# Moving the tiles that TensorE streams to one address residue in an attention and two-layer MoE kernel

## The chip, the cores and the metric

The kernel runs on one core of a Trainium2 chip. The time is the device time of one execution in microseconds (us). TensorE (PE) does the matrix multiplications; each is a weight load (LDWEIGHTS, engine row PEld) of the stationary operand and a MATMUL that streams the moving operand through it into PSUM. VectorE (DVE), ScalarE (ACT) and GpSimd (POOL) do the rest, SyncE (SP) issues the DMAs. SBUF, the working memory, has 128 partitions; an address below is a byte within a partition.

## The reference

All is computed in float32 (the weights are drawn as float64 and come in as pairs of 32-bit words).

```
attention: batch 2, 8 heads, 768 positions, head size 64
  scores = q k^T / 8 within |i-j| < 16, beside q kmax^T / 8 + log 32 for the 24 blocks of 32 keys
  a = softmax over both;  x = a [v, mean of v by block]          -> 1536 tokens x 512
moe:   h = relu(x @ w_in);  y = (h * h) @ w_out                  w_in 512 x 2048, w_out 2048 x 512
moe2:  h = y @ w_in2;  e = exp(h - max);  s = h * e / (sum e + 1e-9)
       ln = (s - mean) / sqrt(var + 1e-6) * g;  out = ln @ w_out2   w_in2 512 x 1024, w_out2 1024 x 512
```

## The kernel before, in words

To keep float32 precision, each operand of a large product is split in two parts of type float32r, a high part (`xh`, `gh`, `yh`, `lh`, and half 0 of a weight tile) and what is left (`xl`, `gl`, `yl`, `ll`, half 1). A product is then three matmuls: high by high, high by low, low by high.

The 1536 tokens are three tiles of 512. A string, `ORDER`, sets by hand in which order every engine gets its work; the letters M, U, G, D, O name the five stages of one step of the first MoE layer. There are 48 steps: 3 token tiles by 16 chunks of 128 hidden columns.

- M, `mm1` (line 466): 12 matmuls into one PSUM bank `h`. Stationary are slices of `wi`, 128 columns each; moving are `xh`, `xl`, 512 columns each, in the order xh, xl, xh for each quarter of the 512 inputs.
- U, G, D: the ReLU into `r`, the squares `gh` (line 481) and `r` (line 482) on ACT, and `gl` = r - gh on DVE or POOL (line 89).
- O, `mm2` (line 495): 12 matmuls into four PSUM banks `acc`, three in each. Stationary are slices of `wo`; moving are gh, gl, gh.

The attention of tokens tiles still to come (lines 181 to 360) lies between the first steps, until about 162 us. The weights come by DMA as 64-bit words into `st`, are put together as float32 in `wf` by ACT and DVE (letters a to e), and split into the ring `wp` (`wi`, `wo`; letters F, f). The weights of the second MoE layer go through the same path: ten 128 x 2 x 512 tiles into `w2` of a pool `rp` that is opened once the attention's tiles are given back, the next two into a `wi` slot of the ring, the last six into `wo` slots.

The second layer works on 12 blocks of 128 tokens, in the function `moe2`:

- `ysplit` (ACT, POOL) makes `yh`, `yl` in slots of `wf`;
- `mm3` (line 541): 2 x 12 matmuls into two banks; stationary are slices of yh, yl, moving are eight `w2` tiles (named `w` in the profile);
- `solu` (lines 548 to 566): a chain over DVE, ACT and POOL;
- `ln_tr` (line 578): 8 transposes, and the split into `lh`, `ll`;
- `mm4` (line 601): 24 matmuls into one bank `po`. Stationary are lh, ll; moving are the weights: 6 matmuls with `w2` (`w` in the profile), 6 with the ring slot `wi`, 12 with `wo`. The last block does it in two halves of 256 columns.

Tiles come from pools. A pool of the left side is put behind the one opened before it; pools of the right side are put down from the end of the memory. `gp` holds r, gh, gl (two slots each) and the small tiles of `solu` (three slots each). Tiles start on multiples of 32 bytes.

Of the kernel before, what the change touches and what calls it, by code (L numbers as in the profile page):

```python
# [12 lines left out]
F32 = mybir.dt.float32  # L13
# [46 lines left out]
def attn_moe_kernel(ctx, tc, q, k, v, w_in, w_out, w2_in, w2_out, g_ln, out):  # L60
# [5 lines left out]
    P = 128  # L66
# [28 lines left out]
    one = cp.tile([P, 1], F32, name="one")  # L95
    g_sb = cp.tile([P, NF2], F32, name="g_sb")

    gp = ctx.enter_context(tc.tile_pool(name="gp", bufs=3))
    yp = ctx.enter_context(tc.tile_pool(name="yp", bufs=1))
    wp = ctx.enter_context(tc.tile_pool(name="wp", bufs=RING))  # L100
    stp = ctx.enter_context(tc.tile_pool(name="stp", bufs=3))
# [15 lines left out]
    rctx = ExitStack()  # L117
    ctx2 = ExitStack()
    rp = {}
# [424 lines left out]
    def solu(i):  # L544
        h2 = h2_t.pop(i)
        yhl.pop(i)
        nm = gp.tile([P, 1], F32, name="nm")
        nc.vector.reduce_max(out=nm, in_=h2, axis=AX.X, negate=True)  # L548
        e = stp.tile([P, DF2], F32, name="st")
        s = gp.tile([P, 1], F32, name="s2")  # L550
        nc.scalar.activation(out=e, in_=h2, func=AF.Exp, bias=nm, accum_out=s)  # L551
        nc.vector.tensor_tensor(out=e, in0=h2, in1=e, op=ALU.mult)
        st = gp.tile([P, 2, 6], F32, name="bst")
        for n in range(2):
            nc.vector.bn_stats(out=st[:, n], in_=e[:, n * 512:(n + 1) * 512])
        mv = gp.tile([P, 2], F32, name="mv")
        nc.vector.bn_aggr(out=mv, in_=st)
        rs = gp.tile([P, 1], F32, name="rs")
        nc.vector.tensor_scalar(out=rs, in0=s, scalar1=1e-9, scalar2=None, op0=ALU.add)
        nc.vector.reciprocal(out=rs, in_=rs)  # L560
        vr = gp.tile([P, 1], F32, name="vr")
        nc.vector.tensor_scalar(out=vr, in0=mv[:, 1:2], scalar1=rs, scalar2=rs, op0=ALU.mult, op1=ALU.mult)
        nc.vector.tensor_scalar(out=vr, in0=vr, scalar1=1e-6, scalar2=None, op0=ALU.add)  # L563
        nc.gpsimd.tensor_tensor(out=vr, in0=vr, in1=mhalf, op=ALU.pow)  # L564
        nc.vector.tensor_tensor(out=vr, in0=vr, in1=rs, op=ALU.mult)
        nc.vector.tensor_scalar(out=e, in0=e, scalar1=mv[:, 0:1], scalar2=vr, op0=ALU.subtract, op1=ALU.mult)
        u_t[i] = e

    def moe2():
# [36 lines left out]
        for i in range(1, NY + 4):  # L606
            if i < NY:
                mm3(i, 0)
                mm3(i, 1)
                if i + 2 < NY:  # L610
                    ysplit(i + 2)
            if 2 <= i < NY + 2:
                ln_tr(i - 2)
            if i < NY:
                solu(i)
            if 3 <= i < NY + 3:
                mm4(i - 3)


    def start():  # L620
        consts()
        for i in range(NVB):
            nc.vector.memset(vw[i][0:WK, 0, :], 0.0)
        for i in range(NKB):
            nc.gpsimd.memset(kT[i][:, 0:16], 0.0)
            nc.gpsimd.memset(kT[i][:, S + 16:S + 32], 0.0)
# [10 lines left out]
    def load_g(n):  # L637
# [21 lines left out]
        "Ya": lambda s: y_out(s, 0), "Yd": lambda s: y_out(s, 1),  # L659

        "z": ysplit, "u": solu, "i": lambda nh: mm3(0, nh),
    }
    LAST = f"X{len(units) - 1}"

    with tc.manual_schedule():
        start()
        for tok in ORDER.split():
            op, n, e = re.fullmatch(r"([A-Za-z]+)(\d+)([adp]?)", tok).groups()
            if tok == "i0":
                rp["h2", 0] = ctx2.enter_context(tc.tile_pool(name="ps_m0", bufs=1, space=PSUM, side="right", reuse_waits="tile"))  # L670
            OPS[op](int(n), *([e] if e else []))
            if tok == LAST:
                actx.close()
                rp["p"] = rctx.enter_context(tc.tile_pool(name="rp", bufs=1, side="right", reuse_waits="tile"))
        lctx.close()
        psctx.close()
        moe2()
        rctx.close()
        ctx2.close()
# [30 lines left out]
```

## Time and profile before

| | us |
|---|---|
| median of 3 runs | 522.45 |
| lowest, highest | 522.23, 525.81 |
| profiled execution: device time | 522.28 |
| profiled execution: span of its instructions | 520.1 |
| TensorE busy | 493.1 |
| DVE, ACT, POOL busy | 352.4, 236.7, 126.9 |
| mean granted TensorE clock | 0.986 of full speed |

Busy time of TensorE is no measure of how fast it streams, since a matmul's record overlaps the next one. How fast it streams is read from the starts: the time from the start of a run of matmuls to the start of what follows, divided by their number.

### The profile page before, as it was taken

How to read it: one execution, taken by the hardware profiler on the slowest of the kernel's cores; microseconds unless marked ns; L12 is line 12 of the kernel's file. 1: busy time of each engine (PE TensorE's matmuls, PEld its weight loads, DVE VectorE, ACT ScalarE, POOL GpSimd, SP SyncE). 2: the span in 40 equal slices, each digit the busy share in tenths (PEclk: the TensorE clock that was granted, in tenths of full speed). 3: DMA queues.
4: the chain of work that ended last, by engine and by line, in shares of the span. 5: the costliest groups of instructions: out<-in, count | busy, mean ns of one | idle time of the engine just before them, and what ended most of it. 6: DMA issues, size and time to landing. Idle time of an engine off the chain costs nothing.

```text
span 520.1 us, 8025 instructions
## 1 busy us (share of the span) xinstructions
PE 493.1 (95%) x2990; PEld 406.0 (78%) x2990; DVE 352.4 (68%) x748; ACT 236.7 (46%) x526; POOL 126.9 (24%) x137
## 2 busy tenths in 40 slices
PE   6786797999999999999999999999999999999997
PEld 5775676787788888888888888888777888888886
DVE  3998989698971669952017969869177877665560
ACT  2465776679673444242335545465422242222231
POOL 2222444331210126101114144232312111210000
PEclk9898989999999999999999999999999999999999
DMA  9989789474810042450000414321000001000001
GB/s 178 239 201 191 178 188 208 102 181 132 195 44 0 2 137 66 125 159 0 0 1 0 162 42 129 109 95 73 0 2 0 21 20 42 20 22 20 21 39 42
DMA packets 59590, 44.03 MB, mean 85 GB/s; under 512 B 46624, under 2 KB 49184, under 8 KB 59552
## 3 DMA queue, kind: packets, MB, share of 16 engines
q1 hardware_dynamic: 59552, 43.53, 33.0%
q8 instruction: 23, 0.38, 0.3%
q14 instruction: 15, 0.12, 0.1%
HBM read 39.19 MB, written 3.15 MB: 81 GB/s over the span
## 4 chain that ended last, share of the span: by engine, by line
PE 78%; DVE 8%; issue 5%; DMA 3%; SPq 3%; ACT 1%; POOL 1%; POOLq 0%
PE h L466 24%; PE acc L495 24%; PE po L601 13%; PE h L541 9%; DMA kl<-in_k_dram 2%; PE lt L578 2%; PE at L347 2%; PE at L287 1%; PE at L332 1%; SPq L199 1%; DMA vw<-vs 1%; DVE vs L258 1%; DVE sm L308 1%; PE h L296 1%; PE at L207 1%
## 5 line engine op out<-in xcount | busy, mean ns | idle before, releaser
L495 PE MATMUL acc<-gh,wo 128*128 128x512 f32 x384 | 129.3, 398 | 0.0
L466 PE MATMUL h<-xh,wi 128*128 128x512 f32 x384 | 128.7, 396 | 0.0
L466 PEld LDWEIGHTS h<-xh,wi 128*128 128x128 f32 x384 | 72.7, 189 | 17.0 <-DVE pt L629 0.2
L495 PEld LDWEIGHTS acc<-gh,wo 128*128 128x128 f32 x384 | 72.3, 188 | 17.4 <-issue 0.2
L495 PE MATMUL acc<-gl,wo 128*128 128x512 f32 x192 | 76.0, 396 | 0.0
L466 PE MATMUL h<-xl,wi 128*128 128x512 f32 x192 | 76.0, 396 | 0.0
L89 POOL TENSOR_TENSOR gl<-r,gh 128x512 fp32r<-128x512 f32 x29 | 40.0, 1378 | 143.8 <-ACT r L482 101.7
L541 PE MATMUL h<-w,wf 128*128 128x512 f32 x288 | 69.6, 395 | 0.7 <-POOL wf L89 0.6
L541 PEld LDWEIGHTS h<-w,wf 128*128 128x128 f32 x288 | 53.7, 187 | 14.7 <-POOL wf L89 1.1
L481 ACT ACTIVATE gh<-r 128x512 fp32r<-128x512 f32 x48 | 30.3, 631 | 58.4 <-DVE r L475 47.7
L399 ACT ACTIVATE wf<-st 128x512 f32<-128x512 f32 x48 | 31.8, 667 | 27.6 <-DMA st<-in_moe_w_in_dram 16.5
L475 DVE TENSOR_SCALAR r<-h 128x512 f32<-128x512 f32 x22 | 15.1, 687 | 42.5 <-PE h L466 38.2
L495 PEld LDWEIGHTS acc<-gl,wo 128*128 128x128 f32 x192 | 36.0, 188 | 8.3
L466 PEld LDWEIGHTS h<-xl,wi 128*128 128x128 f32 x192 | 36.4, 189 | 7.6
L316 ACT ACTIVATE sm<-sm,mn 128x120 f32<-128x120 f32 x96 | 36.5, 382 | 8.1 <-DVE mn L308 8.1
L551 ACT ACTIVATE st<-h,nm 128x1024 f32<-128x1024 f32 x12 | 13.4, 1117 | 55.7 <-DVE nm L548 55.7
L416 DVE SCALAR_TENSOR_TENSOR wf<-st,wf 128x512 uint32<-128x512 uint32 x48 | 37.9, 797 | 1.1
L413 DVE SCALAR_TENSOR_TENSOR wf<-st,wf 128x512 uint32<-128x512 uint32 x48 | 33.9, 711 | 0.9
L564 POOL TENSOR_TENSOR vr<-vr,mhalf 128x1 f32<-128x1 f32 x12 | 6.6, 552 | 113.0 <-DVE vr L563 113.0
L473 ACT ACTIVATE r<-h 128x512 f32<-128x512 f32 x26 | 15.5, 595 | 39.6 <-PE h L466 39.5
L482 ACT ACTIVATE r<-r 128x512 f32<-128x512 f32 x48 | 30.4, 633 | 1.5
L601 PE MATMUL po<-wo,lh 128*128 128x512 f32 (+1 forms) x104 | 30.0, 373 | 0.0
(112 smaller groups left out, 793.2 us busy)
## 6 DMA issues: line engine op xcount, KB each, us to landing
st<-in_moe_w_out_dram SPq DMA_DIRECT2D x24, 512.0 KB, 4.2
st<-in_moe_w_in_dram SPq DMA_DIRECT2D x32, 256.0 KB, 4.0
st<-in_moe_w_in_dram SPq DMA_DIRECT2D x8, 512.0 KB, 3.7
kl<-in_v_dram SPq DMA_DIRECT2D x8, 384.0 KB, 5.1
kl<-in_k_dram SPq DMA_DIRECT2D x16, 192.0 KB, 4.1
out_dram<-ob SPq DMA_DIRECT2D x11, 256.0 KB, 2.0
vw<-in_v_dram SPq DMA_DIRECT2D x16, 168.0 KB, 2.9
qr<-in_q_dram SPq DMA_DIRECT2D x16, 128.0 KB, 4.2
```

The source lines that it names most:

```text
L89: eng.tensor_tensor(out=lo, in0=x, in1=hi.bitcast(F32), op=ALU.subtract)
L316: nc.scalar.activation(out=sm[:, j], in_=sm[:, j], func=AF.Exp, bias=mn[:, j:j + 1], scale=-1.0, accum_out=su[:, j:j + 1])
L399: nc.scalar.activation(out=wf_t[n], in_=st_t[n].rearrange("p (n t) -> p n t", t=2)[:, :, 1], func=AF.Abs)
L413: nc.vector.scalar_tensor_tensor(out=w, in0=st[:, :, 0], scalar=29, in1=w, op0=ALU.logical_shift_right, op1=ALU.bitwise_or)
L416: nc.vector.scalar_tensor_tensor(out=w, in0=st[:, :, 1], scalar=0xC0000000, in1=w, op0=ALU.bitwise_and, op1=ALU.bitwise_or)
L466: nc.tensor.matmul(ps, wi[:, wsel, d, :], x[t][:, d, :], start=(n == 0), stop=(n == 3 * HP - 1))
L473: nc.scalar.activation(out=r_t[s], in_=h_t.pop(s), func=AF.Relu)
L481: nc.scalar.activation(out=gh, in_=r, func=AF.Square)
L482: nc.scalar.activation(out=r, in_=r, func=AF.Square)
L495: nc.tensor.matmul(acc_t[e], wo[:, wsel, e, :], x, start=(edge(s, -1) and i == 0), stop=(edge(s, 1) and i == 2))
L541: nc.tensor.matmul(h2[:, fs], x[:, c, :], w_t[NW1 + nh * NDC + c][:, wsel, :], start=(n == 0), stop=(n == 3 * NDC - 1))
L601: nc.tensor.matmul(po[:, ds], x[:, cs], w_t[NW1 + 8 + c][:, wsel, ds], start=(n == 0), stop=(n == 3 * NF2 - 1))
```

## The change

It moves tiles and nothing else. The six small tiles of `solu` go from `gp` to a pool `sp` of their own, which is opened ahead of `gp`, so that r, gh and gl stand 672 bytes further on. A pool of one tile of 304 float32 values (1216 bytes), which nothing writes or reads, is opened on the right side before `rp`, so that `rp` stands 1216 bytes lower. Every instruction, its engine and its place in its engine's order stay as they are. Where the tiles stand in the two programs as built:

```
tile                                   first byte before      now       remainder by 2048: before, now
r                                            18560           19232            128    800
gh  (two slots of 2048 bytes)                22656           23328            128    800
gl  (two slots)                              26752           27424            128    800
small tiles of solu                          30848           18560
y of token tile 0                            31520           31520            800    800
ring: wi (3 slots), wo (6 slots)      39712, 64288    39712, 64288            800    800
st, wf (yh, yl are in wf slots)       88864, 101152   88864, 101152           800    800
xh, xl (3 tiles each)                113440, 138016  113440, 138016           800    800
lh, ll (in the place of xh)          113440, 121632  113440, 121632           800    800
rp: y of token tiles 1, 2                   172000          170784           2016    800
rp: w2 (10 tiles of 4096 bytes)             188384          187168           2016    800
```

By 128 these remainders are 0 (128), 32 (800) and 96 (2016). All slices that a matmul takes of these tiles begin at multiples of 512 bytes from the tile's start. Since `rp` now lies on other tiles of the attention, which are given back, the GpSimd instructions that write three of the low halves of `w2` wait for other DMAs of the attention than before; no other wait changes.

```diff
-    gp = ctx.enter_context(tc.tile_pool(name="gp", bufs=3))
+
+    sp = ctx.enter_context(tc.tile_pool(name="sp", bufs=3))
+    gp = ctx.enter_context(tc.tile_pool(name="gp", bufs=2))
...
-        nm = gp.tile([P, 1], F32, name="nm")
+        nm = sp.tile([P, 1], F32, name="nm")
...
-        s = gp.tile([P, 1], F32, name="s2")
+        s = sp.tile([P, 1], F32, name="s2")
...
-        st = gp.tile([P, 2, 6], F32, name="bst")
+        st = sp.tile([P, 2, 6], F32, name="bst")
...
-        mv = gp.tile([P, 2], F32, name="mv")
+        mv = sp.tile([P, 2], F32, name="mv")
...
-        rs = gp.tile([P, 1], F32, name="rs")
+        rs = sp.tile([P, 1], F32, name="rs")
...
-        vr = gp.tile([P, 1], F32, name="vr")
+        vr = sp.tile([P, 1], F32, name="vr")
...
                 actx.close()
+                rp["pad"] = rctx.enter_context(tc.tile_pool(name="pad", bufs=1, side="right"))
+                rp["pad"].tile([P, 304], F32, name="pad")
                 rp["p"] = rctx.enter_context(tc.tile_pool(name="rp", bufs=1, side="right", reuse_waits="tile"))
```

## Rows read from the trace of the kernel before

**Rows 1.** The page: busy us of each engine; the chain's shares by line.

```profile
PE 493.1 (95%) x2990; PEld 406.0 (78%) x2990; DVE 352.4 (68%) x748; ACT 236.7 (46%) x526; POOL 126.9 (24%) x137
...
PE h L466 24%; PE acc L495 24%; PE po L601 13%; PE h L541 9%; DMA kl<-in_k_dram 2%; PE lt L578 2%; PE at L347 2%; PE at L287 1%; PE at L332 1%; SPq L199 1%; DMA vw<-vs 1%; DVE vs L258 1%; DVE sm L308 1%; PE h L296 1%; PE at L207 1%
```

**Rows 2.** Stretches: from:to, length, busy us (x instructions) by engine, PEclk, DMA.

```profile
161.80:350.90 189.10, 189.10 (x816) 152.98 (x815) 117.29 (x183) 83.21 (x137) 52.52 (x38) 1.00 0.23 71
350.90:366.80 15.90, 15.33 (x65) 11.78 (x64) 12.97 (x20) 10.20 (x18) 5.20 (x5) 1.00 0.15 61
...
375.00:397.00 22.00, 21.67 (x102) 17.21 (x100) 17.60 (x28) 4.48 (x7) 3.64 (x4) 1.00 0.00 1
397.00:510.00 113.00, 113.00 (x533) 92.84 (x532) 73.98 (x121) 32.51 (x48) 14.27 (x17) 1.00 0.06 24
```

**Rows 3.** Stretches, line 495 (`mm2`) alone: PE, PEld busy.

```profile
91.00:161.80 70.80, 24.11 (x96) 17.51 (x96) 0.99 0.49 120
161.80:350.90 189.10, 103.41 (x420) 78.77 (x419) 1.00 0.23 71
```

**Rows 4.** The same for line 466 (`mm1`).

```profile
161.80:350.90 189.10, 96.38 (x396) 74.21 (x396) 1.00 0.23 71
```

**Rows 5.** Chain of waits in order of time: start us, us, what.

```profile
95.87 2.80 PE acc L495 x12
...
124.22 2.75 PE h L466 x12
...
184.39 2.76 PE h L466 x12
187.15 2.81 PE acc L495 x12
...
402.71 5.61 PE h L541 x24
...
409.19 5.50 PE po L601 x24
```

**Rows 6.** PE's timeline, `mm1` then `mm2`: start us, us, what (out<-moving,stationary).

```profile
301.27 0.40 PE L466 MATMUL h<-xh,wi 128*128 128x512 f32 x1
...
303.12 0.62 PE L466 MATMUL h<-xh,wi 128*128 128x512 f32 x2
...
304.03 0.40 PE L495 MATMUL acc<-gh,wo 128*128 128x512 f32 x1
...
305.91 0.40 PE L495 MATMUL acc<-gh,wo 128*128 128x512 f32 x1
```

**Rows 7.** PE's timeline, one `mm4`; here out<-moving,stationary with lh, ll stationary.

```profile
409.73 0.63 PE L601 MATMUL po<-w,lh 128*128 128x512 f32 x2
...
410.43 0.62 PE L601 MATMUL po<-wi,lh 128*128 128x512 f32 x2
...
411.81 0.62 PE L601 MATMUL po<-wo,lh 128*128 128x512 f32 x2
...
414.53 5.77 PE L541 MATMUL h<-w,wf 128*128 128x512 f32 x24
```

**Rows 8.** Timeline; in brackets the engine's idle time before and what ended it.

```profile
332.15 0.60 ACT L473 ACTIVATE r<-h 128x512 f32<-128x512 f32 x1 [2.56 <-PE h L466]
...
350.93 2.59 DVE L511 TENSOR_TENSOR y<-acc,y 128x512 f32<-128x512 f32 x4 [0.83 <-PE acc L495]
...
366.88 2.59 PE L541 MATMUL h<-w,wf 128*128 128x512 f32 x10 [0.62 <-POOL wf L89]
...
375.09 1.22 DVE L548 TENSOR_REDUCE nm<-h 128x1 f32<-128x1024 f32 x1 [6.47 <-PE h L541]
...
396.10 1.09 PE L578 MATMUL lt<-ident,st 128*128 128x128 f32 x8 [0.24 <-DVE ll L89]
```

**Rows 9.** Tile `w`: duration ns min/median/max, first and last start us.

```profile
L89 POOL TENSOR_TENSOR w<-wf,w x6: 1305/1365/1487, 299.3 to 342.0; 128x512 fp32r<-128x512 f32 x6
```

**Rows 10.** SP's timeline: the last load of the attention.

```profile
131.27 0.86 SPq L241 DMA_DIRECT2D vw<-vs  x1
```

## The prediction

> **What bounds the kernel now.** Read the busy times and the chain of waits first: TensorE is busy for 493.1 of 520.1 us, and four matmul lines, `mm1`, `mm2`, `mm4`, `mm3`, hold 70% of the chain [rows 1]. Next the stretches: from 161.8 to 350.9 us and from 397 to 510 us PE is busy without a gap at the full granted clock, 2.4 GHz, while no other engine is above 66% [rows 2]. There the end moves with the interval from one matmul's start to the next, and with nothing else. So the third view is that interval, by the tile that is streamed.
>
> In one `mm1` the last four matmuls start from 303.12 to 304.03 us, 0.2275 us each; the `mm2` that follows takes 1.88 us for its first eight, 0.235 us each [rows 6]. Shape, type and clock are the same. `mm4` shows it within one line, into one PSUM bank, with one stationary tile: three matmuls that stream `w2` take 0.70 us (0.233 each), the six that stream `wi` 1.38 us (0.230), the twelve that stream `wo` 2.72 us (0.2267) [rows 7]. The slow tiles, gh, gl and `w2`, are the ones that leave a remainder of 0 or 96 by 128; the fast ones, xh, `wi` and `wo`, leave 32, as every stationary slice does. `mm1` as a whole takes 2.76 us, though twelve at 0.2267 would be 2.72: its first eight, behind `mm2`, take 1.85 us, 0.231 each, before the pace is reached [rows 5, 6]. So a fast tile has to run in after a slow one, and a slow one never gets there.
>
> The Trainium skill speaks against this reading. TensorE: Matmul & The Clock Gate, "Step-by-step: what each phase is for", says that "Loading the next tile's weights doesn't steal SBUF read bandwidth from the running matmul", and SBUF — State Buffer, "Who interferes with whom", that "PE and ACT never wait on anyone". By that an address could not matter and the time would stay; the trace's 0.2267 beside 0.233 within one line does not agree, unless something other than the address tells those tiles apart. That is a rival below.
>
> **The change, part by part.** No instruction is added or removed and none changes its place, so there are three edits to cost.
>
> (a) *gh, gl (and r) go to remainder 32.* I expect `mm2` to stream at the pace of `wo` in `mm4`, and `mm1` behind it to have nothing to run in from.
> - 161.8 to 350.9 us: 420 matmuls of `mm2` are 35 groups [rows 3], 396 of `mm1` are 33 [rows 4]. A `mm2` goes from 2.81 to 2.72 us, 0.09 less, and a `mm1` from 2.76 to 2.72, 0.04 less [rows 5, 7]. 35 x 0.09 + 33 x 0.04 = 3.15 + 1.32 = **4.5 us**.
> - 91 to 161.8 us: 8 groups of `mm2` [rows 3], mostly behind matmuls of the attention, where also a fast tile runs in: there `mm1` takes 2.75 and `mm2` 2.80 us [rows 5]. 8 x 0.05 = **0.4 us**.
>
> (b) *`w2` goes to remainder 32.* A `mm3` goes from 5.61 to 24 x 0.2267 = 5.44 us, 0.17 less [rows 5, 7]. In `mm4` six matmuls win up to 0.007 us each and the six `wi` behind them 0.02 us together [rows 7]; but the transposes just ahead leave a run-in as the attention does, so I take 0.03 of a bound of 0.06. In 397 to 510 us and behind it stand 8 `mm3` and 12 `mm4`: 8 x 0.17 + 12 x 0.03 = **1.7 us**.
>
> (c) *Other waits, and the moved small tiles.* The low halves of `w2` on POOL that now wait for other loads start at 299.3 us at the earliest, and the last load of the attention was issued at 131.27 us [rows 9, 10]; the cover is 168 us, so nothing. The pad is never touched. Of the moved small tiles the trace shows no price; the instructions on them keep their form, and I take nothing. The bound is nothing below, and above the 0.1 us or so of one short DVE operation in each of the 12 `solu` chains, off PE's path after 397 us.
>
> **What of it reaches the end.** PE pulls ahead of the others by 0.13 us in each pair of `mm1` and `mm2`, so each place where another engine's work gates PE has to be looked at.
> - Until 350.9 us the others wait for PE: ACT for 2.56 us at 332.15, DVE for 0.83 us at 350.93 [rows 8]. Between these two PE wins some 3.4 pairs x 0.13 = 0.44 us, less than the 0.83. The 4.5 us are kept.
> - From 350.93 to 366.88 us DVE is busy for 12.97 of 15.9 us making the last weights, ACT and POOL split y behind it, and the first `mm3` waits for POOL for 0.62 us [rows 2, 8]. PE's 0.3 us there only lengthen that wait: lost, and not in the sum above.
> - 366.88 to 375.09: two half `mm3` and one `mm2` between, about 34 matmuls x 0.007 = **0.2 us**, kept, since DVE then waits for PE for 6.47 us [rows 8].
> - 375 to 397: the first two `solu` chains and y's last sums keep DVE busy for 17.6 of 22 us, and PE waits for `ll` for 0.24 us at its end [rows 2, 8]. Three `mm3` and one `mm2` would win 3 x 0.17 + 0.09 = 0.6 us; lost.
> - From 397 us DVE is busy for 74 of 113 us and PE never waits [rows 2]; the 1.7 us are kept.
>
> Sum: 4.5 + 0.4 + 1.7 + 0.2 = 6.8 us. The profiled execution took 522.28 us (its span 520.1 and 2.2 around it), 0.17 under the median of 522.45. 522.28 - 6.8 = 515.5; beside the median 515.6. I predict **515.6 us**. If the lost 0.9 us were kept too, and no group behind the attention or the transposes had to run in (0.4 + 0.4 us more), 513.9; if each of the 68 groups before 350.9 us kept half a run-in of 0.04, 517.0.
>
> **The rivals.**
> 1. *Every change of tile has to be run in, whatever the remainder.* Then `mm2` gets the length that `mm1` has now, 2.76 us, and `mm1` stays: 35 x 0.05 + 8 x 0.05 = 2.15, `mm3` wins 0.14 x 8 = 1.1: 3.3 us, **519.1**. For it: `mm1` does begin slow behind `mm2`. Against it: `wi` to `wo` in `mm4` is such a change of tile, and `wo` keeps 0.2267 over all twelve [rows 7]. Chance 0.08.
> 2. *`mm2` is slow because it goes round four PSUM banks*, `w2` because of its place. Then only (b) acts: 1.7 + 0.15, **520.6**. Against it: `mm3` and `mm4` are as slow on `w2` within a bank. Chance 0.08.
> 3. *The place in memory counts, not the remainder*: gh, gl and `w2` lie at the two ends, below 31 KB and above 184 KB, the fast tiles between them, and the change moves them by a kilobyte. Then nothing changes: **522.4**. For it: in this trace the two explanations go together for each tile. Against it: both ends are slow by nearly the same 0.007 us, and a run-in of several matmuls looks like two streams that find a phase, which is a matter of low address bits. Chance 0.13. The two rules of the Trainium skill quoted above would end here as well.
> 4. *Slower.* ACT, DVE and POOL now write gh, gl and r at the same remainder at which PE reads xh, and the pace of xh, `wi`, `wo` breaks: 33 x 0.04 for `mm1` at 2.80 us, and 12 x 18 x 0.007 for `mm4` = 1.3 + 1.5, with gh and `w2` staying slow: 2.8 us, **525.2**. It decides where (a) and (b) together bring less than these 2.8 us. Against it: already now the ring and `wf` are written at remainder 32 beside every `mm1`, and PE has no gap in that stretch [rows 2]. Chance 0.04.
>
> **The numbers.** The forecast has a chance of 0.67; its own range is 513.9 to 517.0. With rivals 1 and 2 the range 513.8 to 520.8 holds 0.67 + 0.16, less a little for the forecast's edges: about 0.8. About 1%, 5.2 us, is what a measurement of this kernel tells from no change. Faster by over 1% means under 517.2: the forecast, 0.67. Rivals 1, 2, 3 and nearly all of 4 stay within 1%: 0.31. Slower by over 1%, 0.02, is rival 4 with something more.
>
> **What would show it.** In the changed profile: `mm2` 2.72 us and `mm1` 2.72 us in the chain, without a run-in at the start; `mm3` 5.44; the three `w` matmuls in `mm4` at the pace of `wo`; the wait for POOL near 362 us longer than 0.62 and that for `ll` longer than 0.24; the rest at the same lengths. Wrong it would be by a `mm2` still at 2.81 (rival 2 or 3, told apart by `mm3`), by a `mm1` still at 2.76 (rival 1), or by PE waits that grow elsewhere and give the 6.8 us back.

## The result, and the profile after

The changed kernel takes 515.18 us, the median of 4 runs (514.84 to 515.69); the kernel before took 523.1 us (522.23 to 525.81, 4 runs, the three of the first table among them). The ratio is 0.9841, with a 95% interval of 0.9802 to 0.988. 515.6 was predicted. Thirteen later runs of the kernel before gave 521.92, so 523.1 is on the high side; against 521.92 the changed kernel would be 6.7 us faster, not 7.9. The profiled execution took 514.84 us, its span 512.7 us, at the same mean clock as before, 0.986.

The page of the changed kernel: busy us of each engine, then the chain's shares by line (`mm1` is now line 468, `mm2` 497, `mm3` 543, `mm4` 603).

```profile
PE 485.4 (95%) x2990; PEld 405.5 (79%) x2990; DVE 349.5 (68%) x748; ACT 236.0 (46%) x526; POOL 127.0 (25%) x137
...
PE acc L497 21%; PE h L468 21%; PE po L603 13%; PE h L543 8%; DMA st<-in_moe_w_in_dram 4%; PE lt L580 2%; DMA vw<-vs 2%; SPq L201 2%; DVE vs L260 1%; DMA kl<-in_v_dram 1%; PE at L349 1%; DMA kl<-in_k_dram 1%; SPq L174 1%; ACT sm L318 1%; ACT wf L401 1%
```

The same 2990 matmuls keep PE busy for 7.7 us less, while ACT and POOL stay within a microsecond and DVE is busy for 2.9 us less, for which no cause is shown [rows 1]. The busy share tells nothing: it is 95% in both. The loads of the weights (`st`) have come into the chain, beside the attention.

The chain in time: start us, us, what.

```profile
188.35 2.72 PE h L468 x12
191.07 2.72 PE acc L497 x12
...
403.30 5.46 PE po L603 x24
408.76 5.44 PE h L543 x24
```

Beside [rows 5]: `mm1` 2.76 to 2.72 us, `mm2` 2.81 to 2.72, `mm3` 5.61 to 5.44, `mm4` 5.50 to 5.46.

PE's timeline, one `mm1` with the `mm2` behind it, and one `mm4`: start us, us, what (out<-moving,stationary).

```profile
296.99 0.39 PE L468 MATMUL h<-xh,wi 128*128 128x512 f32 x1
...
298.80 0.62 PE L468 MATMUL h<-xh,wi 128*128 128x512 f32 x2
...
299.71 0.39 PE L497 MATMUL acc<-gh,wo 128*128 128x512 f32 x1
...
302.43 0.39 PE L468 MATMUL h<-xh,wi 128*128 128x512 f32 x1
...
403.84 0.61 PE L603 MATMUL po<-w,lh 128*128 128x512 f32 x2
...
404.52 0.61 PE L603 MATMUL po<-wi,lh 128*128 128x512 f32 x2
...
405.88 0.61 PE L603 MATMUL po<-wo,lh 128*128 128x512 f32 x2
...
408.60 0.61 PE L543 MATMUL h<-w,wf 128*128 128x512 f32 x2
```

The first eight matmuls of this `mm1` take 298.80 - 296.99 = 1.81 us, 0.2263 each, where they took 1.85 [rows 6]; `mm2` takes 2.72 for its twelve. In `mm4` the three of `w` take 0.68 us, the six of `wi` 1.36, the twelve of `wo` 2.72: 0.2267 each, all three [rows 7]. There is one pace left, and no run-in where neither neighbour is slow.

### The profile page after: what moved, and what is told of

Its sections match the earlier page's. It is cut to its first block, busy times and chain, and to the rows that moved or that the text cites. A ratio compares the mean times of both kernels' runs of the same rounds, so it can differ in the third digit from the quotient of the medians.

```text
span 512.7 us, 8027 instructions
## 1 busy us (share of the span) xinstructions
PE 485.4 (95%) x2990; PEld 405.5 (79%) x2990; DVE 349.5 (68%) x748; ACT 236.0 (46%) x526; POOL 127.0 (25%) x137
## 4 chain that ended last, share of the span: by engine, by line
PE 68%; DVE 8%; DMA 8%; issue 5%; SPq 5%; ACT 4%; POOL 1%; ACTq 0%; POOLq 0%
PE acc L497 21%; PE h L468 21%; PE po L603 13%; PE h L543 8%; DMA st<-in_moe_w_in_dram 4%; PE lt L580 2%; DMA vw<-vs 2%; SPq L201 2%; DVE vs L260 1%; DMA kl<-in_v_dram 1%; PE at L349 1%; DMA kl<-in_k_dram 1%; SPq L174 1%; ACT sm L318 1%; ACT wf L401 1%
## 5 line engine op out<-in xcount | busy, mean ns | idle before, releaser
L497 PE MATMUL acc<-gh,wo 128*128 128x512 f32 x384 | 126.6, 391 | 0.0
L497 PE MATMUL acc<-gl,wo 128*128 128x512 f32 x192 | 74.8, 389 | 0.0
L543 PE MATMUL h<-w,wf 128*128 128x512 f32 x288 | 67.8, 390 | 1.4 <-POOL wf L89 0.6
L418 DVE SCALAR_TENSOR_TENSOR wf<-st,wf 128x512 uint32<-128x512 uint32 x48 | 40.5, 850 | 1.1
L415 DVE SCALAR_TENSOR_TENSOR wf<-st,wf 128x512 uint32<-128x512 uint32 x48 | 34.1, 713 | 0.9
```

Source lines behind the costliest of these rows:

```text
L415: nc.vector.scalar_tensor_tensor(out=w, in0=st[:, :, 0], scalar=29, in1=w, op0=ALU.logical_shift_right, op1=ALU.bitwise_or)
L418: nc.vector.scalar_tensor_tensor(out=w, in0=st[:, :, 1], scalar=0xC0000000, in1=w, op0=ALU.bitwise_and, op1=ALU.bitwise_or)
L497: nc.tensor.matmul(acc_t[e], wo[:, wsel, e, :], x, start=(edge(s, -1) and i == 0), stop=(edge(s, 1) and i == 2))
L543: nc.tensor.matmul(h2[:, fs], x[:, c, :], w_t[NW1 + nh * NDC + c][:, wsel, :], start=(n == 0), stop=(n == 3 * NDC - 1))
```

## Where the 7.4 us of span lie

First the stretch beside the attention, from one and the same `mm2` to one and the same `mm1`, before and after: length, then busy us of PE, PEld, DVE, ACT, POOL; then the PE clock and the DMA.

```profile
95.62:161.91 66.29, 66.04 (x639) 53.05 (x638) 52.97 (x173) 46.86 (x137) 12.60 (x11) 1.00 0.50 123
```

```profile
94.69:160.99 66.30, 65.75 (x639) 53.05 (x638) 52.94 (x173) 46.65 (x137) 12.69 (x11) 1.00 0.49 122
```

Then the same four places behind it, by PE's timeline: of the kernel before,

```profile
161.91 0.40 PE L466 MATMUL h<-xh,wi 128*128 128x512 f32 x1
...
359.76 0.40 PE L495 MATMUL acc<-gh,wo 128*128 128x512 f32 x1
...
396.95 0.71 PE L601 MATMUL po<-w,lh 128*128 128x512 f32 x2
...
511.15 0.40 PE L601 MATMUL po<-w,lh 128*128 128x256 f32 x2
```

and of the changed one.

```profile
160.99 0.39 PE L468 MATMUL h<-xh,wi 128*128 128x512 f32 x1
...
354.11 0.39 PE L497 MATMUL acc<-gh,wo 128*128 128x512 f32 x1
...
391.26 0.70 PE L603 MATMUL po<-w,lh 128*128 128x512 f32 x2
...
503.68 0.40 PE L603 MATMUL po<-w,lh 128*128 128x256 f32 x2
```

| stretch | before | after | gained | predicted |
|---|---|---|---|---|
| start to 95.62 / 94.69 | 95.62 | 94.69 | 0.93 | 0 |
| to the first `mm1` without attention ahead of it | 66.29 | 66.30 | 0.0 | 0.4 |
| to the last `mm2` before the second layer | 197.85 | 193.12 | 4.73 | 4.5 |
| to the first `mm4` | 37.19 | 37.15 | 0.04 | 0.2 |
| to the last half block | 114.20 | 112.42 | 1.78 | 1.7 |

From the start of that half block to its end the changed kernel takes longer. The last block's `mm4` is done in 48 matmuls of 256 columns, the only ones of that width in the second layer. They start from 511.15 to 516.73 us before and from 503.68 to 509.31 us after:

```profile
516.73 0.28 PE L601 MATMUL po<-wo,ll 128*128 128x256 f32 x1
```

```profile
509.31 0.28 PE L603 MATMUL po<-wo,ll 128*128 128x256 f32 x1
```

That is 5.58 us before and 5.63 after for 47 intervals, 0.1187 and 0.1198 us each. Twelve of the 48 stream `w2`; the other 36 stream tiles that haven't moved. At this width the change costs a little, which the prediction didn't see; the experiment with moved stationary tiles comes back to it.

The 0.93 us at the start can't be put down to the change: the start differs by more than that between the versions below. The `mm1` that starts at 161.91 and 160.99 here starts between 158.46 and 163.50 in them, though their edits, too, only move tiles; and one program alone, part (b) below, took from 517.59 to 522.1 us in ten runs. The granted clock goes some way with it: over the first 95 us its mean is 0.98 in the three profiles with the earliest start (158.46, 158.60, 158.67) and 0.91 to 0.96 in the others. Before and after it is 0.93 in both, so it doesn't explain these 0.93 us. From that `mm1` to the last half block is what can be compared: 349.24 us before, 342.69 after, 6.55 less; predicted for it were 6.4.

The waits of the changed kernel by the timeline; in brackets the idle time before and what ended it.

```profile
345.47 2.56 DVE L513 TENSOR_TENSOR y<-acc,y 128x512 f32<-128x512 f32 x4 [0.37 <-PE acc L497]
...
361.36 2.58 PE L543 MATMUL h<-w,wf 128*128 128x512 f32 x10 [0.62 <-POOL wf L89]
...
369.41 1.22 DVE L550 TENSOR_REDUCE nm<-h 128x1 f32<-128x1024 f32 x1 [6.30 <-PE h L543]
...
384.33 5.69 PE L543 MATMUL h<-w,wf 128*128 128x512 f32 x24 [0.48 <-DVE st L554]
...
390.42 1.09 PE L580 MATMUL lt<-ident,st 128*128 128x128 f32 x8 [0.39 <-DVE ll L89]
```

DVE's wait for PE has shrunk from 0.83 to 0.37 us [rows 8], 0.46 less where 0.44 were to be gained in those pairs: with as much again DVE would set the pace there. Later, ahead of the first `mm4`, PE waits 0.48 us for `st` and 0.39 for `ll`, 0.63 more than the 0.24 before [rows 8]: the 0.6 us of three `mm3` and a `mm2` that the prediction gave up for lost.

## The experiments

The prediction's arithmetic held, but its reading of the addresses rested on three remainders only. **Theory 1** takes it by the word: a streamed tile's own remainder by 128 is good (32) or bad (0, 96). **Theory 2**: what counts is the streamed tile against the stationary one of the same matmul; 32 was good since every stationary slice had it too. Beside them stand the prediction's rivals: a run-in at every change of tile, the PSUM banks, the place in memory, and the writers at the same remainder. The first three kernels have four to ten timings, beside 13 of the kernel before (521.92 us, 520.53 to 523.38). The others have one time and one profile each; there the lengths of the groups decide, not the total with its uneven start.

**Part (a) alone.** The changed kernel without the pad: gh, gl at 800 by 2048, `w2` again at 2016.

```diff
-                rp["pad"] = rctx.enter_context(tc.tile_pool(name="pad", bufs=1, side="right"))
-                rp["pad"].tile([P, 304], F32, name="pad")
```

> Part (a) alone: the small tiles go ahead of gp as in the change, the 1216-byte pad is left out, so gh and gl stand at remainder 32 by 128 and w2 stays at 96. If the remainder decides, mm1 and mm2 take 2.72 us each, mm3 stays at 5.60 and mm4 at 5.50; the stretch before 350 us gives 4.7 us and the one after 397 us nothing: about 517.1 us. If w2's place or tile changes as such mattered (a run-in at each edge), mm1 would stay at 2.76. The 0.9 us that the changed kernel was ahead already before its first mm1 and mm2 pair without attention (161.91 before, 160.99 after): if it is by gh, it is here too; if it varies from run to run, it need not be.

Measured: 517.35 us (515.08 to 517.77, 4 runs), ratio 0.9893 (0.9864 to 0.9922). The chain:

```profile
202.26 2.72 PE acc L497 x12
204.98 2.72 PE h L468 x12
...
421.41 5.60 PE h L543 x24
```

`mm2` and `mm1` have the new pace, `mm3` the old one. `mm2` still goes round its four PSUM banks, so the banks weren't it (rival 2), and `mm1` has lost its run-in, though `mm2` streams other tiles (rival 1).

**Part (b) alone.** The kernel before with the pad's two lines and nothing else.

```diff
+                rp["pad"] = rctx.enter_context(tc.tile_pool(name="pad", bufs=1, side="right"))
+                rp["pad"].tile([P, 304], F32, name="pad")
```

> Part (b) alone: the pad of 1216 bytes, so w2 stands at remainder 32, and gh, gl stay at 0. If the remainder decides, mm1 stays at 2.76 and mm2 at 2.81, mm3 takes 5.44 and mm4 5.46; 1.8 to 1.9 us less than before: about 520.6 us by the median of before as first shown. If w2 were slow by its place near the end of the memory, mm3 would stay at 5.60 and the time at 522.5.

Measured: 519.62 us (517.59 to 522.1, 10 runs), ratio 0.9959 (0.9938 to 0.9981).

```profile
202.71 2.76 PE h L466 x12
205.47 2.81 PE acc L495 x12
...
415.98 5.44 PE h L541 x24
```

The other half: `mm3` is fast, the first layer as before. From the first undisturbed `mm1` to the last half block part (a) gains 4.65 us (161.30 to 505.89) and part (b) 1.84 (163.50 to 510.90); together 6.5, and both at once gave 6.55. They don't touch each other.

**All tiles 96 bytes further.** gh, gl, xh, the ring, `wf`, lh, ll and `w2` all start at 896 by 2048, a remainder of 0 by 128, at which gh was slow.

```diff
+    cp.tile([P, 24], F32, name="shift")
     sp = ctx.enter_context(tc.tile_pool(name="sp", bufs=3))
...
-                rp["pad"].tile([P, 304], F32, name="pad")
+                rp["pad"].tile([P, 280], F32, name="pad")
```

> The changed kernel with every tile that PE streams or loads moved on by 96 bytes together (96 unused bytes at the start, the pad shortened by as much): all stand at 896 by 2048, which is 0 by 128, where gh was slow. Theory 1, the remainder of the streamed tile alone decides and 32 is a good one: every matmul of 512 columns goes at 0.233 us, mm1 and mm2 2.80, mm3 and mm4 5.60, about 8 us more than the changed kernel, 523.5 us. Theory 2, streamed and stationary tile must have the same remainder: 2.72, 2.72, 5.44, 5.46 as in the changed kernel, 515.2 us.

Measured: 514.39 us (512.59 to 515.77, 4 runs), ratio 0.9854 (0.9828 to 0.988).

```profile
202.28 2.72 PE h L469 x12
205.00 2.72 PE acc L498 x12
...
412.68 5.46 PE po L604 x24
418.13 5.45 PE h L544 x24
```

Everything is as fast as at 800. Theory 1 falls: no remainder is good by itself.

**The stationary tiles 96 bytes further.** The opposite move: `st`, `wf` (with yh, yl), xh, xl, lh, ll go to 896, the ring, gh, gl and `w2` stay at 800.

```diff
+    pb = ctx.enter_context(tc.tile_pool(name="pb", bufs=1))
+    pb.tile([P, 24], F32, name="shift")
     stp = ctx.enter_context(tc.tile_pool(name="stp", bufs=3))
```

> The changed kernel with st, wf, xh, xl and so lh, ll moved on by 96 bytes, everything else in place. That moves the stationary tile of mm3 (yh, yl in wf) and of mm4 (lh, ll) against the streamed w2 and ring, and the streamed tile of mm1 (xh, xl) against wi; mm2 keeps both. If the distance between the two counts, whichever is moved: mm3 5.60, mm4 about 5.60, mm1 about 2.80 and mm2 2.72 to 2.76 behind it; about 522 to 523 us. If only the streamed tile counted, mm3 and mm4 would stay at 5.44 and 5.46.

Measured: 520.07 us. The groups came out as expected; the total is 2 to 3 us less, and its first undisturbed `mm1` starts at 158.46, 2.53 us earlier than in the changed kernel.

```profile
203.08 2.81 PE h L470 x12
205.89 2.76 PE acc L499 x12
...
411.34 5.62 PE h L545 x24
417.83 5.63 PE po L605 x24
```

The parts are exchanged: `mm1`, whose xh now stands 96 bytes off its `wi`, takes 2.81 us, and `mm2`, whose gh and `wo` agree, takes the 2.76 of a fast group behind a slow one. `mm3` and `mm4` are slow with `w2` exactly where it was fast. In `mm4` now all 24 matmuls are off their lh, ll, not six only, and it takes 5.63 instead of 5.46. So it isn't the place of the streamed tile (rival 3) but its distance from the stationary one, whichever of the two is moved: theory 2.

The 256-column matmuls of the last block go the other way. All 48 are 160 bytes off here:

```profile
509.00 0.40 PE L605 MATMUL po<-w,lh 128*128 128x256 f32 x2
...
514.51 0.28 PE L605 MATMUL po<-wo,ll 128*128 128x256 f32 x1
```

From the first start to the last they take 5.51 us, 0.1172 each, where at distance 0 they take 5.63, 0.1198. So what agreement gains is shown for 512 columns; at 256 columns these runs show a small loss.

**What period the distance has.** Theory 2 leaves open by what number the two must agree. Six more kernels move gh and gl against `wo`, with all other pairs kept at distance 0. The first leaves two small tiles of `solu` (nm, bst) ahead of `gp` and takes four into a pool behind it, which puts gh 384 bytes off, 0 by 128.

```diff
+    sq = ctx.enter_context(tc.tile_pool(name="sq", bufs=3))
...
-        s = sp.tile([P, 1], F32, name="s2")
+        s = sq.tile([P, 1], F32, name="s2")
...
-        mv = sp.tile([P, 2], F32, name="mv")
+        mv = sq.tile([P, 2], F32, name="mv")
...
-        rs = sp.tile([P, 1], F32, name="rs")
+        rs = sq.tile([P, 1], F32, name="rs")
...
-        vr = sp.tile([P, 1], F32, name="vr")
+        vr = sq.tile([P, 1], F32, name="vr")
```

> The changed kernel with nm and bst alone ahead of gp and the other four small tiles behind it: r, gh, gl stand at 416 by 2048, which is 32 by 128 but 160 by 256 and 416 by 512; xh, the ring and w2 stay at 800. If the remainder by 128 (or by less) is what counts: mm2 2.72, mm1 2.72, 515.2 us. If it is the remainder by 256 or more: mm2 2.81 and mm1 2.76 as before, about 520 us.

Measured: 517.28 us; about 520 was expected for a slow `mm2`.

```profile
201.99 2.79 PE acc L498 x12
204.78 2.73 PE h L469 x12
```

`mm2` is slow, though by a little less than at 96 bytes (2.79 for 2.81). Agreement by 128 is not enough; the prediction's "by 128" was too short.

256 bytes off: rs and vr go behind `gp`, the tiles from y on stand 64 bytes further, the pad is 64 bytes smaller; gh is at 608, the others at 864.

```diff
+    sq = ctx.enter_context(tc.tile_pool(name="sq", bufs=3))
+    pb = ctx.enter_context(tc.tile_pool(name="pb", bufs=1))
+    pb.tile([P, 16], F32, name="shift")
     yp = ctx.enter_context(tc.tile_pool(name="yp", bufs=1))
...
-        rs = sp.tile([P, 1], F32, name="rs")
+        rs = sq.tile([P, 1], F32, name="rs")
...
-        vr = sp.tile([P, 1], F32, name="vr")
+        vr = sq.tile([P, 1], F32, name="vr")
...
-                rp["pad"].tile([P, 304], F32, name="pad")
+                rp["pad"].tile([P, 288], F32, name="pad")
```

> The changed kernel with r, gh, gl 256 bytes below the remainder of all other tiles that PE reads (608 and 864 by 2048). The slices that PE loads step by 512 bytes, so a distance of 512 is known to be harmless. If distances count by 256: mm2 2.72 and mm1 2.72 us. If they count by 512: mm2 about 2.80 and mm1 2.73 to 2.76 us, as with the distance of 384 bytes.

Measured: 512.95 us.

```profile
202.65 2.72 PE h L471 x12
205.37 2.72 PE acc L500 x12
```

Fast. With 128 slow and 256 fast, the distance counts by 256 bytes, among the distances tried.

32 bytes off (and, in the next run, 64: `[P, 16]` and `[P, 288]`):

```diff
+    pb = ctx.enter_context(tc.tile_pool(name="pb", bufs=1))
+    pb.tile([P, 8], F32, name="shift")
     yp = ctx.enter_context(tc.tile_pool(name="yp", bufs=1))
...
-                rp["pad"].tile([P, 304], F32, name="pad")
+                rp["pad"].tile([P, 296], F32, name="pad")
```

> The same with 32 bytes of distance (800 and 832). If streamed and stationary tile have to stand at exactly the same remainder: mm2 about 2.80, mm1 up to 2.76 us, 519 us. If a small distance is tolerated, because it is only a matter of which part of the memory both reads touch at a time: 2.72 and 2.72.

> The same with 64 bytes of distance (800 and 864). Exact remainder needed: mm2 about 2.80. Tolerated: 2.72, and then, together with the distances of 32, 96 and 128 bytes seen already, it shows where the tolerance ends.

Measured: 517.65 and 516.26 us. The chains' `mm2`, at 32 bytes:

```profile
201.72 2.80 PE acc L499 x12
```

and at 64 bytes.

```profile
205.98 2.80 PE acc L499 x12
```

Both nearly as slow as at 96; there is no slope towards 0 down to here. So the last two go closer: gh and gl become parts of one tile, begun 16 bytes into it and, in the next run, 4 (`+ 1` for `+ 4`); the other tiles go to 1056 by 2048. That also changes how the program tells gh's slots apart; PE has no gap over 0.02 us between 165 and 345 us in either run, so no new wait shows there.

```diff
+    pb = ctx.enter_context(tc.tile_pool(name="pb", bufs=1))
+    pb.tile([P, 56], F32, name="shift")
...
+    ghl = []
...
-        gh = gp.tile([P, TB], F32R, name="gh", bufs=2)
-        gl = gp.tile([P, TB], F32R, name="gl", bufs=2)
+        if not ghl:
+            ghl.append(gp.tile([P, 4 * TB + 8], F32R, name="ghl", bufs=1))
+        gh = ghl[0][:, s % 2 * TB + 4:s % 2 * TB + TB + 4]
+        gl = ghl[0][:, (2 + s % 2) * TB + 4:(2 + s % 2) * TB + TB + 4]
...
-                rp["pad"].tile([P, 304], F32, name="pad")
+                rp["pad"].tile([P, 240], F32, name="pad")
```

> The changed kernel with gh and gl as parts of one tile, begun 16 bytes into it, and all other tiles that PE reads at a distance by 256 of 16 bytes below that. At 32 bytes mm2 was slow at 2.80 us. If the remainder has to agree to the byte: 2.80 here too, mm1 2.74. If it counts in units of 32 bytes: 2.72.

> The same with gh and gl begun 4 bytes, one element, into the tile. Agreement to the byte needed: mm2 2.80. A unit of 8, 16 or 32 bytes: 2.72.

Measured: 516.6 and 521.51 us. At 16 bytes:

```profile
201.33 2.78 PE acc L502 x12
```

and at 4.

```profile
205.05 2.84 PE acc L502 x12
207.89 2.73 PE h L471 x12
```

One float32 beside full agreement makes the slowest `mm2` of all, 2.84 us or 0.2367 for each matmul, while the `mm1` behind it loses only 0.01. The 521.51 us hold a late start as well (first undisturbed `mm1` at 163.05). All runs together, by the distance of the streamed from the stationary tile (modulo 256; us of a group in the chain):

| distance by 256 | group, kernel | us for 12 matmuls |
|---|---|---|
| 0 | `mm2`: changed, part (a), all 96 further, 256 off; `mm1`: the same | 2.72 |
| 0 | `mm3`: changed, part (b), all 96 further | 2.72 (half of 5.44, 5.45) |
| 0, behind a slow group | `mm1`: before, gh 4 to 128 off; `mm2`: stationary 96 further | 2.73 to 2.76 |
| 4 | `mm2` | 2.84 |
| 16 | `mm2` | 2.78 |
| 96 | `mm2` before; `mm1`, stationary 96 further | 2.81 |
| 128 | `mm2` | 2.79 |
| 160 | `mm3`, stationary 96 further | 2.81 (half of 5.62) |
| 192 | `mm2`, 64 off; `mm3` before | 2.80; 2.80 (half of 5.605, from start to start) |
| 224 | `mm2`, 32 off | 2.80 |

The group behind a slow one carries part of the loss, so `mm1` and `mm2` together are the fairer measure. From start to start the pair takes 5.44 us at distance 0, 5.53 at 16 and 128 bytes, 5.54 at 192, 5.55 at 224, and 5.57 at 4 and at 96.

## Why the prediction was right

- **What bounds the kernel.** Right: the gain lies where PE has no gap, in the interval of the matmuls, and nowhere else.
- **Term (a), 161.8 to 350.9 us, 4.5 us.** From the first undisturbed `mm1` to DVE's sum that starts at 350.93 before and at 345.47 after, 4.54 were measured. The 4.73 of the table go up to the last `mm2`, 9 us further; of what came on top, 0.13 went back just before the first `mm3`. A `mm2` won 0.09 us and a `mm1` 0.04, as put in.
- **Term (a), 91 to 161.8 us, 0.4 us. This step failed.** Between the two profiles PE is busy 0.29 us less in that stretch, but the length stayed (66.29, 66.30): PE's gaps grew from 0.25 us to 0.55, in waits for ACT and DVE at the attention's steps, before and after:

```profile
122.41 1.22 PE L287 MATMUL at<-kw,qT 64*64 64x120 f32 x32 [0.25 <-ACT pt L632]
```

```profile
121.31 1.28 PE L289 MATMUL at<-kw,qT 64*64 64x120 f32 x32 [0.33 <-ACT pt L634]
...
145.98 0.62 PE L334 MATMUL at<-ident,sm 128*120 128x128 f32 x4 [0.22 <-DVE pt L631]
```

The prediction took the whole gain as kept there: its "until 350.9 us the others wait for PE" rested on rows at 332 and 350 us. The other kernels say how far one pair of profiles carries. The same stretch takes 66.58 (part (a)), 66.05 (all 96 further) and 65.86 us (256 off) where `mm2` is fast too, 66.18 to 66.34 in the six kernels, the one before among them, whose gh is 16 to 128 bytes off, and 67.11 at 4 bytes. Against the 66.29 before, the four fast kernels gain from -0.3 to 0.4 us, 0.1 on average: the 0.4 isn't there as a rule, and neither is its loss to these waits. The sum was made up by the 0.93 us of the start, which nobody had predicted and which isn't shown to be the change's. That the total came within half a microsecond is luck to that extent.
- **Term (b), 1.7 us.** 1.78 measured: `mm3` 0.17 by the chain, as put in, `mm4` 0.04 instead of 0.03. Behind the transposes the second and third interval are still 0.2325 and 0.231 us; from the fourth on the pace is 0.227.
- **366.88 to 375.09 us, 0.2 us.** 8.21 us became 8.05, from 361.36 to 369.41: 0.16 kept.
- **What was given up for lost** was lost, at the places named: 0.6 us in waits for DVE between 375 and 397 us, and most of the 0.3 before the first `mm3`. The wait for POOL there stayed at 0.62 us, though the prediction's signs had it growing; instead PE waited 0.29 us for ACT just ahead of it.
- **The reading of the addresses** gave the right forecast on too little: "32 by 128" was neither a good remainder nor the right period. It worked because the change makes the tiles agree by 2048, and so by 256. Tiles put at 416, which also leave 32 by 128, would have been forecast fast, and were slow.
- **The rivals.** 1 to 3 fell with parts (a) and (b) alone and the two moves by 96 bytes. 4 is excluded by the result: gh, gl and r are written at the remainder at which PE reads, and no undisturbed group of 512-column matmuls is slower. The last block's 256-column matmuls are, by 0.05 us in all; they run behind the last write of gh, so they are no sign of rival 4.

The rule of the Trainium skill that spoke against the change, in TensorE: Matmul & The Clock Gate, "Step-by-step: what each phase is for" (loading the next tile's weights takes no read bandwidth from the running matmul), led to "an address could not matter", and that doesn't agree with these runs: with engine, instructions and order the same, the interval goes from 0.2267 to 0.2367 us by the distance between the two tiles that PE itself reads. The prediction read too much into the other rule, in SBUF — State Buffer, "Who interferes with whom" (PE never waits on anyone): it is about one engine against another, and no run here shows PE slowed by another engine's reads or writes.

Why the distance counts stays open. That the streamed reads and the weight loads meet each other would fit, but no run here shows it, nor which two would meet, a matmul's own or the next one's weights, nor why a group has to run in behind a slow one.

## What to carry to other kernels

Where PE has no gap, read the interval between starts by the tile that is streamed, not the busy time; a difference of 3% within one shape and clock is worth a look at the addresses. Let the streamed tile and the stationary slices agree by 256 bytes, by ordering pools or leaving bytes out; a shift of both together costs nothing. Here small tiles between the big ones, and a pool put down from the end of the memory, were the reason why they didn't. All this holds for 128 x 512 matmuls of float32r, each with a weight load of its own; at 256 columns agreement cost 2% (0.1198 for 0.1172 us). Before adding up such a gain, ask for every stretch whether the others wait for PE: some 0.3 us beside the attention and 0.6 us behind the first layer came back as waits.

## What the runs showed of the hardware that was not expected

- At the full granted clock a 128 x 512 float32r matmul with a weight load of its own starts every 0.2267 us when streamed and stationary tile agree by 256 bytes, and every 0.2317 (16 bytes off) to 0.2367 us (4 bytes off) when they don't. The loss is not graded by the distance: 16 to 128 bytes cost 0.06 to 0.09 us in twelve, 4 bytes 0.12; with the run-in of the group behind, 0.09 to 0.13.
- The pace carries over: a group at distance 0 that follows a slow one takes up to 0.04 us longer, and none of that when its neighbours agree too. The run-in is longest behind the slow groups at 96 bytes, 0.04, and shortest at 4 bytes, 0.01.
- At 256 columns the sign turns: 48 matmuls at distance 0 start every 0.1198 us, and every 0.1172 us when all are 160 bytes off.
- Writes of other engines at the same remainder bring no loss that shows: in the run with all tiles 96 bytes further, ACT, DVE and POOL write gh, gl and r at the remainder at which PE reads, and PE keeps 2.72 us in each undisturbed group, as for `wo` in `mm4`, when none of them is written.
